# Weight sums in small pieces between products, a reordered start, and a conversion whose last step is put off

## The chip, the cores and the metric

The kernel runs on one core of one Trainium2 chip. Times are device microseconds (us) of one execution. A profile is one execution, taken by the hardware profiler. Engine names in it: PE is TensorE (matrix products), PEld its weight loads, DVE is VectorE, ACT is ScalarE, POOL is GpSimd, SP issues DMAs. `L406` is a line of the kernel of that run, so the same operation has another line number in another kernel; each part below gives the names.

A ratio is the mean time of one kernel's fast runs over that of the other's fast runs of the same rounds on the same chip. It is not quite the ratio of the medians that stand beside it.

## The reference, cut to what matters

```python
# attention: batch 8, heads 8, sequence 576, head size 64; no softmax
scores = q @ k.T / 8 ; ret = scores * decay(h) ** (i - j) for j <= i ; o = ret @ v
# bridge: x is (4608, 512)
# feed-forward with three first weights and a maximum
h   = max(x @ w1, x @ w2, x @ w3)        # 512 -> 768
out = h @ w_out                          # 768 -> 512
```

The weights arrive as 64-bit floats and have to be converted on the chip; all arithmetic is fp32.

## The kernel before

Attention runs in 36 chunks of 128 rows, each with steps transposes, scores (products s and kv) and values (products o). The feed-forward runs in 9 tiles of 512 tokens. Tile 0 uses plain products ("up", "down") while the weights are still being converted. Tiles 1 to 8 use a Strassen-like scheme of seven products per "unit" (a pair of weight blocks, 9 units in a tile) and of seven products for the last matrix (dx, dy, dz). That scheme needs sums of weight blocks (T), of the last weight (To), and of hidden blocks (H).

A unit, cut. Note that product 3 adds into the PSUM tile `x` that the sum after product 5 reads:

```python
product(5, x, False)
nc.vector.tensor_tensor(c22, x[:], p7[:], op=ALU.add)     # L434: VectorE must read x ...
yield
product(4, z, False)
...
product(3, x, False)                                      # ... before this may start
```

The conversion of one piece of a weight, cut:

```python
nc.vector.tensor_scalar(out=expo, in0=high, scalar1=0x7FF00000, op0=bitwise_and)   # mask
nc.scalar.activation(mant, low, Identity, ...)
nc.scalar.activation(expo, expo, Relu, ...)
nc.vector.tensor_scalar(out=frac, in0=high, scalar1=0xFFFFF, op0=bitwise_and)      # mask
nc.scalar.activation(expo, expo, Relu, ...)
nc.vector.scalar_tensor_tensor(out=mant, in0=frac, ..., in1=mant)
nc.vector.scalar_tensor_tensor(out=expo, in0=high, ..., in1=expo)                  # "finish"
nc.gpsimd.tensor_tensor(w, mant, expo, op=mult)                                    # the weight
```

The sums of the last weight and of the hidden blocks stood in one run at the end of a unit:

```python
nc.vector.tensor_tensor(t1, b12, b11, op=subtract)        # 128x768 each
nc.vector.tensor_tensor(t2, b22, t1, op=subtract)
nc.gpsimd.tensor_tensor(b12, b22, b12, op=subtract)
nc.gpsimd.tensor_tensor(t4, b21, t2, op=subtract)
```

## Time and profile before

| | before |
|---|---|
| median of 3 runs | 856.88 us (856.82 to 857.43) |
| TensorE busy | 97% |
| first up product starts | 31.54 us |
| first down product starts | 108.96 us |
| first product of tile 1 | 139.00 us |
| last product ends | 851.86 us |

The table is a set of milestones on TensorE. Because TensorE is nearly always busy, a change shows as the distance between two milestones growing or shrinking. The first up products, from TensorE's timeline (start, duration, operation, count, idle time before and what ended it):

```profile
31.54 7.13 PE L461 MATMUL up<-xT,w 128*128 128x512 f32 x16 [0.43 <-DVE xT L218]
```

Two groups of the conversion are needed later. The view is the groups of instructions by line; columns are count, then busy us and mean ns of one, then idle time before:

```profile
L273 DVE TENSOR_SCALAR frac<-bits 128x512 int32<-128x512 int32 x24 | 25.7, 1071 | 0.0
...
L268 DVE TENSOR_SCALAR expo<-bits 128x512 int32<-128x512 int32 x24 | 13.3, 556 | 0.0
```

The two masks do the same work, and yet one takes twice the time of the other. In the old order GpSimd's product of the piece before is running when frac comes.

### The profile page before, as it was taken

Reading aid. Unit: us, or ns where it says so; the run is one execution under the profiler, and the core shown is the slowest. Engines: PE = TensorE matmul, PEld = TensorE weight load, DVE = VectorE, ACT = ScalarE, POOL = GpSimd, SP = SyncE. Lnnn points to the kernel's source line nnn. Section 1 sums busy time; section 2 is a strip of 40 time slices with the busy share of each in tenths; the row PEclk is TensorE's granted clock in tenths of the full one; section 3 lists DMA queues with packets and bytes.
Section 4 is the critical chain, followed back from the end, with each engine's and each line's share of the span. In section 5 each row is a group of like instructions: output and inputs, shape, how many; then the busy total and the mean of one; then the engine's idle time right before and its main releaser. Section 6 shows DMA issues by size and latency. Waiting matters only on the chain.

```text
span 855.4 us, 12581 instructions
## 1 busy us (share of the span) xinstructions
PE 831.4 (97%) x4608; PEld 669.8 (78%) x4608; DVE 448.2 (52%) x803; ACT 172.8 (20%) x391; POOL 189.4 (22%) x178
## 2 busy tenths in 40 slices
PE   7999989799999999999999999999999999999998
PEld 5645546678888888888888888888888888888887
DVE  4899945745445544555454535554355535543341
ACT  2555631111011111111111111111111111111211
POOL 3534423423302211111211121112021201201000
PEclk9999999989999999999999999999999999999999
DMA  9655531333023322334133323332333223301001
GB/s 245 171 151 160 182 65 51 55 55 75 17 59 74 59 54 54 55 58 83 49 57 54 64 67 55 56 55 68 66 56 54 49 61 69 58 13 38 1 1 49
DMA packets 232509, 59.06 MB, mean 69 GB/s; under 512 B 213504, under 2 KB 230912, under 8 KB 232448
## 3 DMA queue, kind: packets, MB, share of 16 engines
q1 hardware_dynamic: 232016, 57.74, 30.2%
q8 instruction: 36, 0.59, 0.3%
q10 hardware_dynamic: 432, 0.53, 0.2%
q14 instruction: 25, 0.20, 0.1%
HBM read 48.76 MB, written 9.44 MB: 68 GB/s over the span
## 4 chain that ended last, share of the span: by engine, by line
PE 79%; DVE 8%; SPq 5%; ACT 4%; issue 3%; DMA 1%; POOL 0%; DVEq 0%
PE x L406 26%; PE z L406 12%; PE dx L342 9%; PE y L406 6%; PE dz L342 5%; PE s L181 4%; SPq L141 4%; PE o L211 4%; PE o L216 3%; PE kv L192 3%; PE dy L342 2%; PE down L452 2%; ACT expo L271 2%; ACT expo L275 1%; DVE expo L279 1%
## 5 line engine op out<-in xcount | busy, mean ns | idle before, releaser
L406 PE MATMUL x<-S,T 128*128 128x256 f32 x576 | 147.9, 379 | 0.0
L406 PEld LDWEIGHTS x<-S,T 128*128 128x128 f32 x576 | 109.1, 190 | 15.4 <-ACT u L411 0.3
L151 POOL TENSOR_TENSOR vd<-vraw,gk 128x512 f32<-128x512 f32 x36 | 38.6, 1072 | 350.9 <-DMA vraw<-in_v_dram 315.7
L406 PE MATMUL x<-S,w 128*128 128x256 f32 x288 | 76.2, 387 | 8.6 <-DVE h L434 8.5
L434 DVE TENSOR_TENSOR tmp<-x,p 128x256 f32<-128x256 f32 x48 | 20.4, 425 | 104.8 <-PE x L406 104.8
L406 PE MATMUL x<-xT,w 128*128 128x256 f32 x288 | 74.9, 382 | 0.0
L406 PE MATMUL z<-xT,T 128*128 128x256 f32 x288 | 74.0, 379 | 0.0
L406 PE MATMUL y<-xT,w 128*128 128x256 f32 x288 | 73.9, 379 | 0.0
L406 PE MATMUL z<-S,w 128*128 128x256 f32 x288 | 73.9, 379 | 0.0
L411 ACT COPY p<-x 128x256 f32<-128x256 f32 x72 | 26.8, 372 | 223.1 <-PE x L406 217.9
L184 DVE TENSOR_TENSOR st<-s,causal 128x512 f32<-128x512 f32 x72 | 46.3, 685 | 44.1 <-PE s L181 44.1
L406 PEld LDWEIGHTS x<-S,w 128*128 128x128 f32 x288 | 49.9, 191 | 24.0 <-DVE h L434 11.1
L461 PE MATMUL up<-xT,w 128*128 128x512 f32 x144 | 63.5, 594 | 0.4 <-DVE xT L218 0.4
L218 DVE TENSOR_TENSOR xT<-o,gq 128x512 f32<-128x512 f32 x36 | 24.8, 689 | 70.1 <-PE o L216 64.2
L406 PEld LDWEIGHTS y<-xT,w 128*128 128x128 f32 x288 | 54.7, 190 | 7.4
L406 PEld LDWEIGHTS z<-S,w 128*128 128x128 f32 x288 | 54.7, 190 | 7.5
L406 PEld LDWEIGHTS z<-xT,T 128*128 128x128 f32 x288 | 53.9, 189 | 8.4 <-ACT p L411 0.3
L406 PEld LDWEIGHTS x<-xT,w 128*128 128x128 f32 x288 | 51.6, 191 | 6.6 <-issue 0.8
L324 POOL TENSOR_TENSOR H<-h 128x256 f32<-128x256 f32 x24 | 22.7, 947 | 150.3 <-DVE h L446 150.3
L461 PEld LDWEIGHTS up<-xT,w 128*128 128x128 f32 x144 | 26.7, 190 | 30.9 <-issue 29.9
L181 PEld LDWEIGHTS s<-qT,kT 64*128 64x128 f32 x576 | 37.2, 198 | 13.9 <-issue 11.4
L424 DVE TENSOR_TENSOR tmp<-y,p 128x256 f32<-128x256 f32 x48 | 20.4, 425 | 51.7 <-PE y L406 51.7
(91 smaller groups left out, 1229.6 us busy)
## 6 DMA issues: line engine op xcount, KB each, us to landing
bits<-in_moe_w_dram SPq DMA_DIRECT2D x18, 512.0 KB, 3.7
out_dram<-osb SPq DMA_DIRECT2D x36, 256.0 KB, 2.1
kraw<-in_k_dram SPq DMA_DIRECT2D x32, 256.0 KB, 3.1
vraw<-in_v_dram SPq DMA_DIRECT2D x32, 256.0 KB, 3.5
qraw<-in_q_dram SPq DMA_DIRECT2D x448, 16.0 KB, 1.8
kxraw<-in_k_dram SPq DMA_DIRECT2D x448, 16.0 KB, 1.8
bits<-in_moe_w_out_dram SPq DMA_DIRECT2D x6, 512.0 KB, 3.5
qraw<-in_q_dram SPq DMA_DIRECT2D x7, 256.0 KB, 4.6
```

Source lines behind the costliest of these rows:

```text
L141: nc.sync.dma_start(t[32 * a:32 * a + 32, :, blk, :], src[b, a // 2::2, pos:pos + 32, 32 * (a % 2):32 * (a % 2) + 32].rearrange("p j i -> ...
L151: nc.gpsimd.tensor_tensor(t[:], raws.pop(("v", g))[:], gk[:].unsqueeze(2).to_broadcast([C, H, D]), op=ALU.mult)
L181: nc.tensor.matmul(s[j][:, p, :], lhsT=kT[r, p, :], rhs=qT[r, p, :], start=True, stop=True)
L184: nc.vector.tensor_tensor(st[:, j], s[j][:], masks[start_of(g)][:].unsqueeze(1).to_broadcast([C, NP, C]), op=ALU.mult)
L192: nc.tensor.matmul(kv[:, p, :], lhsT=pair(kr, p)[r:], rhs=pair(vds[g], p)[r:], start=True, stop=True)
L211: nc.tensor.matmul(o[D * j:D * (j + 1), p, :], lhsT=vr[:, 2 * p + j, :], rhs=st[:, j, p, :], start=(p == 0), stop=(old == 0 and p == NP - ...
L216: nc.tensor.matmul(o[:, p, :old], lhsT=sd[:, p, :], rhs=qT[:, p, :old], start=False, stop=(p == NP - 1), skip_group_check=True)
L218: nc.vector.tensor_tensor(xT[t][:, :, i * C:(i + 1) * C], o[:], gq[:], op=ALU.mult)
L342: nc.tensor.matmul(out[:, m, :], lhsT=hS[n](fp)[:, m * P:(m + 1) * P], rhs=late["T"][n][:, fp, :], start=first and m == 0 and fp == 0, sto ...
L406: nc.tensor.matmul(out[:], lhsT=w[:, d * P:(d + 1) * P], rhs=xS[t][n][:, d, :], start=first and d == 0, stop=d == 1, skip_group_check=True)
L411: nc.scalar.copy(c[:], src[:])
L461: nc.tensor.matmul(ps[:], lhsT=w_sb[i, fb][:, dc * P:(dc + 1) * P], rhs=xT[t][:, dc, :], start=(dc == 0), stop=(dc == NDC - 1))
```

## The change

Its intent: no long run of sums in front of an eviction that TensorE waits for; a warm TensorE clock and earlier q, k, v at the start; and masks of the conversion that do not stand beside GpSimd's product.

```diff
+    late, chores = {}, deque()
+    def chore(n=1):
+        for _ in range(min(n, len(chores))): chores.popleft()()
 ... sums_of_outs: three thirds of 128x256, each a VectorE chore and a GpSimd chore
 ... sums_of_hidden: three chores; chore() after products 1, 6 and 5 of a unit
 def product(n, out, first):                      # dx, dy, dz
-    for m in range(NM):
-        for fp in range(NF // 2):
+    for fp in range(NF // 2):
+        for m in range(NM):
 ... conversion, now one generator over all pieces: in its third step
+            if last:
+                (finish of the piece before; its product on GpSimd; load_weights(1))
-                    convert(5 if n < 4 else 4)
+                    convert(7 if i == 0 else 4)
 ... start
+    warm(9)                                      # identity products; warm(5) follows transposes(0)
     load(0); load(1)
+    (gs and gq are loaded here, from another queue)
     load(2)
-    load_weights(1)
     load(3)
-    load_weights(2)
+    load_weights(2); load(4); load_weights(2)
 ...
     scores(2)
-    load(4); values(2); convert(2); scores(3); decay_values(4); convert(2); values(3); convert(4)
+    scores(3); convert(2); values(2); convert(3); decay_values(4); values(3); convert(3)
```

(Before, convert(4) stood after scores(1) as well.) ScalarE also takes over four kT copies from VectorE, the weight loads get four buffers in place of three, and raw q three in place of four.

## The prediction

> **What bounds the kernel now.** I read the page first (busy shares, the 40 slices), then the table of waits of TensorE, then TensorE's timeline, then VectorE's and GpSimd's timelines at each place where TensorE stood still.
>
> ```profile
> PE 831.4 (97%) x4608; PEld 669.8 (78%) x4608; DVE 448.2 (52%) x803; ACT 172.8 (20%) x391; POOL 189.4 (22%) x178
> ...
> PE   7999989799999999999999999999999999999998
> ...
> PEclk9999999989999999999999999999999999999999
> ```
>
> TensorE is the bound nearly everywhere, so the change can only win where TensorE has a hole or runs slowly. The waits name the holes:
>
> ```profile
> PE x L406 <- DVE h L434: 8.5, 6, 6.8
> PE kt L168 <- DMA kraw<-in_k_dram: 5.0, 2, 4.1
> PE down L452 <- POOL w_out L285: 3.0, 2, 1.9
> PE dx L342 <- DVE h L446: 2.0, 8, 0.3
> ```
>
> They cost more than they say, because products after a hole run at half speed. From TensorE's timeline (start, duration):
>
> ```profile
> 164.85 1.03 PE L406 MATMUL z<-xT,T 128*128 128x256 f32 x4
> 172.67 2.08 PE L406 MATMUL x<-S,w 128*128 128x256 f32 x4 [6.80 <-DVE h L434]
> 174.68 2.08 PE L181 MATMUL s<-qT,kT 64*128 64x128 f32 x16
> 176.69 2.07 PE L192 MATMUL kv<-vd,kraw 128*128 128x128 f32 x8
> 178.55 1.07 PE L406 MATMUL x<-xT,w 128*128 128x256 f32 x4
> ```
>
> Four products start every 0.86 us elsewhere, 16 score products take 1.1, 8 kv products 1.0. From 164.85 to 178.55 that would be 0.86 + 0.95 + 1.1 + 1.0 = 3.9 us; it took 13.7. **Hole A costs 9.8 us.** It is in the second token tile, before unit 3. VectorE there:
>
> ```profile
> 162.28 0.94 DVE L297 TENSOR_TENSOR T<-w,w 128x256 f32<-128x256 f32 x1
> 163.25 0.84 DVE L298 TENSOR_TENSOR T<-w,T 128x256 f32<-128x256 f32 x1
> 164.01 1.48 DVE L312 TENSOR_TENSOR To<-w_out 128x768 f32<-128x768 f32 x1
> 165.52 1.36 DVE L313 TENSOR_TENSOR To<-w_out,To 128x768 f32<-128x768 f32 x1
> 166.81 2.02 DVE L322 TENSOR_TENSOR H<-h 128x256 f32<-128x256 f32 x1
> 168.86 1.90 DVE L323 TENSOR_TENSOR H<-H,h 128x256 f32<-128x256 f32 x1
> 170.69 0.70 DVE L162 STREAM_TRANSPOSE kT<-kxraw 128x512 f32<-128x512 f32 x1
> ```
>
> The last seventh-product reuses the PSUM tile that L434 must read first, and L434 stands in line behind all these sums.
>
> Hole B: the last products of the first tile wait for converted last weights. TensorE from 108.96 to 121.43 is 12.5 us; it holds 12 down products of 512 columns (0.43 each, 5.2), 1.1 and 1.0: 7.3. **Hole B costs 5.2 us.** Holes C: eight times dx waits for h (0.25 shown, 0.41 by start-to-start against the neighbours), 3.3 us; five further waits for L434 after hole A (0.25 to 0.65 by starts), 2.5 us. The start: the first large product begins at 31.54, while the attention work before it (four chunks of s 1.1, kv 1.1, o 1.0, three of state 1.1, ten groups of transposes 0.44: 20.5 us warm) began at 4.11 and could have ended about 7 us sooner. All else is back-to-back products.
>
> **What the Trainium skill says.** "SBUF — State Buffer", Who interferes with whom: VectorE and GpSimd share a port pair; a two-port-mode VectorE operation, or one with two SBUF inputs, blocks against a GpSimd operation that reads SBUF, and whoever issues first keeps it. The trace agrees: a mask alone takes 0.42 us, and under a GpSimd product (91.96 to 93.35)
>
> ```profile
> 91.80 0.42 DVE L268 TENSOR_SCALAR expo<-bits 128x512 int32<-128x512 int32 x1
> 92.13 1.50 DVE L273 TENSOR_SCALAR frac<-bits 128x512 int32<-128x512 int32 x1
> ```
>
> "TensorE: Matmul & The Clock Gate", What's actually happening: an idle window of about 3.4 us drops the clock to half. The trace agrees: 6.80 us idle, then 2.08 for 1.03. The same page, Architectural detail: VectorE's queue is strictly first in, first out; that is hole A. "DMA: Bandwidth & Descriptors", Issuing engines are not separate DMA queues: transfers interleave whichever engine issued them; so gq and gs, on ScalarE's queue, delay the first q and k. The trace shows the DMA share at 0.90 in the first 10 us, and no more than that.
>
> **The change part by part.**
> 1. *Last-weight sums and unit sums as chores.* The work stays; the order against the evictions changes. At hole A, VectorE's line from its copy of unit 2 (164.01, end of the T pair) to L434 becomes: transposes 1.24, one third of the last-weight sums (two of 128x256 at about 0.43, and up to 0.9 of GpSimd's weight sums in the way), y eviction 0.3 to 0.4, L434 0.4: done at about 167.0 to 167.9. TensorE needs it at 165.7. I leave a loss of 1.8, and 0.4 for a possible clock dip: saved 9.8 - 2.2 = 7.6 us. The rest of the last-weight sums falls in units 3 and 4, each behind an eviction that has 2 to 4 products' time before the next. In the other tiles the two hidden sums still stand before the critical L434 (the chore slots are after products 1 and 6), but GpSimd's two now come after it: 0.55 + 0.88 (their means) becomes about 0.42 x 2, 0.6 us less, which covers waits of 0.25 to 0.65: saved 2.3 of 2.5.
> 2. *dx with the hidden pair as the outer loop.* The last h is needed after 8 matmul records instead of 4: 4 x 0.216 = 0.86 later, more than 0.41. Saved 3.3 us. This is the surest part.
> 3. *Conversion with the finish put behind the next piece's masks.* Before, 80 steps run between products, and one whole piece and more is left at 108.9; after, 98 of 100 steps are issued by then, and only two STT finishes and one mant lie behind the last product. But VectorE has to do it: 23 pieces between about 29 and 112. Per piece before, from 31.4 to 115.3, 83.9 us less 7.3 (12 maxima) less 7.3 (attention) over 22 pieces: 3.15, with 0.3 of it idle for ScalarE. After, the idle goes; but mant, with two SBUF inputs, now starts beside GpSimd's product, and the mask behind it waits for that product. I estimate 0.69 + 0.69 + 1.3 + 0.4 = 3.08. The last w_out is then ready at about 29 + 1.3 + 22 x 3.08 + 14.6 + 1.3 = 114.0; TensorE asks at 108.96 + 10 x 0.43 = 113.3. A short wait without a clock dip: saved 4.2 of 5.2.
> 4. *The start.* Nine identity products (18 records at the cold 0.27 us) warm the clock from about 1.6 to 6; the transposes then take 0.44 instead of 1.09, and s starts at about 9.1 instead of 10.12, kv at 10.2 instead of 11.8. Without gq, gs and the first weight in front, k, q, v of chunks 0 to 3 come earlier, so attention for chunk 3 and the transposes of chunk 4 end at about 28, not 31. But the first weight is then loaded after chunk 3 and converted only behind scores of chunk 3: after xT of chunk 3 (27.9) still frac 0.33, STT 0.61, and GpSimd's product, which mant holds up, 1.8: 30.8. TensorE then idles nearly 3 us where it was busy. Saved: 31.5 - 30.8 = 0.7 us.
> 5. *kT copies to ScalarE, buffers 4 to 3 for q, WAHEAD 4*: nothing by themselves. The tail (last copy, last store) is unchanged.
>
> Sum: 7.6 + 2.3 + 3.3 + 4.2 + 0.7 = 18.1 us; 856.9 - 18.1 = 838.8, said as 838.5.
>
> **Rivals.**
> - *The conversion becomes the bound in the first tile.* VectorE was busy 71.6 of 77.4 us there. If GpSimd's products block more than I think (3.3 per piece), the last weights come 5 us late with a clock dip, hole B stays, and the time is about 843. Against it: frac's mean before, 1.07 us where 0.42 is the mask alone, says that most products blocked a mask already.
> - *The start gains all of it.* If the first weight lands and converts sooner, up to 2.5 us more: 836. Against it: VectorE's new order puts STT of the first piece behind xT of chunk 3.
> - *Hole A only shrinks and still drops the clock.* A hole of 2 to 3 us with GpSimd's sums behind it costs up to 4: 841. For it: the two holes of 1.14 and 1.90 in hole B were enough to lower the clock to 0.93.
> - *Chores make new holes.* A chore behind product 5's eviction delays z's by up to 0.9 us; z's buffer is not needed for a whole unit. I give it little: +1.
> - *Everything goes right*: 21 us of holes and 2 at the start: 834.
>
> **Range and chances.** The holes sum to 20.8 us outside the start, so under 832 is nearly excluded, and nothing that I see makes it slower. Within 2% ends at 839.7, a saving of 17.1, only 1 us from my sum; the errors of parts 1, 3 and 4 are about 1, 1.7 and 1.2 us, together some 2.5 to 3. So 832.5 to 844.5 for 8 in 10; faster by over 2% 0.62, within 2% 0.37, slower 0.01.
>
> **What would show it.** Part 2: no wait of dx for L446 at all. Part 1: in the second tile one wait of x for L434's successor of 1 to 2.5 us where 6.8 stood, and no half-speed products. Part 3: down's wait for w_out under 1.5 us in all. Part 4: kv of chunk 0 at about 10.2; the first up product at 30 to 32, waiting for GpSimd's w. The mean of the expo mask over 1 us and of frac near 0.4 would show the lock moved from one mask to the other, not gone. I am wrong if TensorE waits for w inside the first tile's up products, or if its clock falls below 0.9 after 20 us.

## The result, and the profile after

The changed kernel took 847.25 us (median of 4 runs, 846.79 to 847.83) beside 857.15 for the kernel before: ratio 0.9882, 95% interval 0.9865 to 0.9899. It is faster by 1.2%, where 2.1% was predicted, and lies outside the predicted range; "within 2%" had been given a chance of 0.37.

| milestone on TensorE, us | before | after | stretch before | stretch after |
|---|---|---|---|---|
| first up starts | 31.54 | 33.40 | 31.54 | 33.40 |
| first down starts | 108.96 | 114.33 | 77.42 | 80.93 |
| thirteenth down record starts (hole B lies in here) | 121.43 | 127.19 | 12.47 | 12.87 |
| last product ends | 851.86 | 841.57 | 730.4 | 714.4 |

So the first tile lost 5.8 us, and everything behind it gained 16.0. TensorE's waits of the changed kernel (who waited for whom: us in total, times, longest):

```profile
PE up L483 <- POOL w L385: 4.7, 1, 4.7
PE down L474 <- POOL w_out L385: 3.4, 2, 2.6
...
PE x L425 <- DVE h L455: 1.4, 2, 0.7
```

The waits of dx for h are gone, the 6.8 us wait of x has become two of 0.7, and a new one of 4.7 us leads the list. At hole A, TensorE's timeline after (L425 is the line of the unit products):

```profile
170.61 1.03 PE L425 MATMUL z<-xT,T 128*128 128x256 f32 x4
172.31 1.13 PE L425 MATMUL x<-S,w 128*128 128x256 f32 x4 [0.67 <-DVE h L455]
173.37 1.16 PE L183 MATMUL s<-qT,kT 64*128 64x128 f32 x16
174.47 1.16 PE L194 MATMUL kv<-vd,kraw 128*128 128x128 f32 x8
175.46 1.03 PE L425 MATMUL x<-xT,w 128*128 128x256 f32 x4
```

The same stretch that took 13.70 us takes 4.85, and nothing in it runs at half speed. The new hole before the first up:

```profile
28.15 0.60 PE L173 MATMUL qt<-ident,qraw 128*128 128x128 f32 x4
33.40 8.83 PE L483 MATMUL up<-xT,w 128*128 128x512 f32 x16 [4.66 <-POOL w L385]
```

Sixteen up records took 7.13 us before; 8.83 here means that the first of them ran at half speed after the hole (the granted clock was 0.81 from 33.4 to 42.2 us). The chain that ended last, followed back, names what stood in front of that product (start, length, what):

```profile
24.67 1.10 PE o L218 x8
...
25.87 0.69 DVE state L199
...
26.89 1.41 DVE frac L375
...
31.03 0.61 DVE expo L379
...
31.70 1.65 POOL w L385
...
33.40 5.41 PE up L483 x8
...
38.84 0.02 ACT h L486
...
39.32 0.77 ACT mant L370
...
40.11 0.04 DVE mant L391
```

Three things are to be seen. VectorE's state update at 25.87 comes after products of values(2) (o L218). The frac mask takes 1.41 us in the chain, beside a GpSimd product. And after the up product, the conversion of the next pieces goes on only when ScalarE has copied that product: the copy stands ahead of `mant` in ScalarE's line. VectorE's own waits:

```profile
DVE expo L369 <- POOL w L385: 16.2, 15, 1.2
...
DVE mant L391 <- ACT mant L370: 5.4, 1, 5.4
DVE expo L369 <- POOL w_out L385: 4.6, 4, 1.2
DVE state L199 <- PE o L218: 2.0, 1, 2.0
```

VectorE waits 20.8 us in all (16.2 + 4.6) for GpSimd's product before the first mask of a piece. No such line exists in the profile before. The groups that answer to those of before:

```profile
L369 DVE TENSOR_SCALAR expo<-bits 128x512 int32<-128x512 int32 x24 | 12.8, 534 | 20.8 <-POOL w L385 16.2 <-POOL w_out L385 4.6
...
L375 DVE TENSOR_SCALAR frac<-bits 128x512 int32<-128x512 int32 x24 | 11.2, 466 | 0.0
```

The frac mask fell from 1071 to 466 ns, so the masks are indeed away from GpSimd's product: because VectorE now stands still until it is done. The 14.5 us that frac gave back came back as 20.8 us of waiting.

### The profile page after: what moved, and what is told of

Read it like the earlier page. It is cut to its first block, busy times and chain, and to the rows that moved or that the text cites. A ratio compares the mean times of both kernels' runs of the same rounds, so it can differ in the third digit from the quotient of the medians.

```text
span 845.1 us, 12652 instructions
## 1 busy us (share of the span) xinstructions
PE 830.1 (98%) x4636; PEld 672.6 (80%) x4636; DVE 414.4 (49%) x803; ACT 175.0 (21%) x395; POOL 189.8 (22%) x182
## 4 chain that ended last, share of the span: by engine, by line
PE 86%; DVE 6%; POOL 4%; issue 1%; SPq 1%; DMA 0%; ACT 0%; DVEq 0%; POOLq 0%
PE x L425 28%; PE z L425 14%; PE dx L312 10%; PE y L425 7%; PE dz L312 5%; PE s L183 4%; PE o L213 4%; PE kv L194 4%; PE o L218 4%; POOL w L385 3%; PE dy L312 2%; PE down L474 2%; DVE expo L379 2%; DVE expo L369 1%; SPq L146 1%
## 5 line engine op out<-in xcount | busy, mean ns | idle before, releaser
L425 PE MATMUL x<-S,T 128*128 128x256 f32 x576 | 147.8, 379 | 0.0
L425 PEld LDWEIGHTS x<-S,T 128*128 128x128 f32 x576 | 109.2, 190 | 15.2
L425 PE MATMUL x<-S,w 128*128 128x256 f32 x288 | 74.6, 381 | 1.4 <-DVE h L455 1.4
L425 PE MATMUL x<-xT,w 128*128 128x256 f32 x288 | 74.8, 382 | 0.0
L425 PE MATMUL z<-S,w 128*128 128x256 f32 x288 | 73.9, 379 | 0.0
L425 PE MATMUL z<-xT,T 128*128 128x256 f32 x288 | 73.9, 379 | 0.0
L425 PE MATMUL y<-xT,w 128*128 128x256 f32 x288 | 73.9, 379 | 0.0
L483 PE MATMUL up<-xT,w 128*128 128x512 f32 x144 | 65.8, 609 | 4.8 <-POOL w L385 4.7
L425 PEld LDWEIGHTS x<-S,w 128*128 128x128 f32 x288 | 49.3, 189 | 15.2 <-DVE h L455 2.4
L425 PEld LDWEIGHTS z<-S,w 128*128 128x128 f32 x288 | 54.7, 190 | 7.4
L425 PEld LDWEIGHTS y<-xT,w 128*128 128x128 f32 x288 | 54.7, 190 | 7.4
L425 PEld LDWEIGHTS z<-xT,T 128*128 128x128 f32 x288 | 54.0, 189 | 8.2
L425 PEld LDWEIGHTS x<-xT,w 128*128 128x128 f32 x288 | 51.5, 190 | 6.6 <-issue 0.8
L295 POOL TENSOR_TENSOR H<-h 128x256 f32<-128x256 f32 x24 | 18.6, 774 | 150.4 <-DVE h L468 150.4
L430 ACT COPY u<-x 128x256 f32<-128x256 f32 x72 | 26.8, 372 | 99.9 <-PE x L425 99.9
```

The source lines that it names most:

```text
L425: nc.tensor.matmul(out[:], lhsT=w[:, d * P:(d + 1) * P], rhs=xS[t][n][:, d, :], start=first and d == 0, stop=d == 1, skip_group_check=True)
L430: nc.scalar.copy(c[:], src[:])
L483: nc.tensor.matmul(ps[:], lhsT=w_sb[i, fb][:, dc * P:(dc + 1) * P], rhs=xT[t][:, dc, :], start=(dc == 0), stop=(dc == NDC - 1))
```

## The experiments

My theory after the result: the sums and the dx order bring some 16 us; the new start and the conversion with the postponed finish give about 6 of it back, through three rings and lines. First, two state tiles: scores(3) now stands before values(2), so the state for chunk 4 has to wait until TensorE has read state 2. Second, two `expo` tiles: the mask of piece n+1 overwrites the tile that GpSimd's product of piece n-1, only just issued, still reads. Third, ScalarE's strict order at the first up. Rivals: the parts need each other, so they cannot be summed; the port shared by VectorE and GpSimd stands behind the tile and would cost the same; the loads set the start.

The control of each ratio is the kernel before, on the same chip. Medians of the kernel before were 857.2 to 859.0 us, so ratios are compared, not medians. The 95% interval of a ratio reaches 0.0013 to 0.0025 to either side; that is 1 to 2 us.

| run | median us | ratio to before | first up | up stretch | hole B stretch |
|---|---|---|---|---|---|
| after | 847.25 | 0.9882 | 33.40 | 80.93 | 12.87 |
| after_again | 848.46 | 0.9888 | 35.04 | 82.20 | 13.33 |
| a_dx | 854.81 | 0.9955 | 31.34 | 77.42 | 12.46 |
| a_sums | 843.05 | 0.9811 | 31.83 | 77.42 | 12.42 |
| b_head_conv | 862.15 | 1.0033 | 33.44 | 81.67 | 12.82 |
| c_state3 | 844.76 | 0.9838 | 31.05 | 80.98 | 13.29 |
| d_expo3 | 846.47 | 0.9847 | 33.70 | 79.10 | 10.06 |
| f_oldconv | 845.11 | 0.9846 | 31.54 | 86.01 | 9.08 |
| h_dveprod | 840.78 | 0.9791 | 33.91 | 79.12 | 7.33 |
| q_oldconv_dve | 849.12 | 0.9888 | 32.08 | 89.82 | 7.33 |
| p_sums_dve | 854.29 | 0.9946 | 37.05 | 82.08 | 15.57 |
| j_early_dve | 837.50 | 0.9755 | 32.47 | 77.42 | 7.33 |
| j_again | 837.43 | 0.9745 | 31.17 | 79.12 | 7.33 |
| k_j_nowarm | 837.28 | 0.9752 | 33.00 | 77.42 | 7.34 |
| m_late_vd | 837.44 | 0.9747 | 31.02 | 79.12 | 7.33 |

("Up stretch" is from the first up to the first down, "hole B stretch" from the first down to the thirteenth down record, both from the profile. 7.33 us of the latter is what it takes without a hole. Every experiment gave correct results.)

### a_sums and b_head_conv: the change in two halves

a_sums is the kernel before with the chores and the dx order alone; b_head_conv is the changed kernel with the old sums and the old dx order.

```diff
 # a_sums, on the kernel before
+ chores, chore() after products 1, 6, 5; dx with fp outside m
 # b_head_conv, on the changed kernel
- chores; dx with fp outside m
+ sums_of_outs, sums_of_hidden in one run, dx with m outside fp
```

> The kernel before with only the two parts that the trace says worked: sums as chores, and dx with the hidden pair outside. Theory (the gain is all in these two, and the new start and conversion give 5 to 6 us of it back): hole A saves 8.9 us, the later tiles 7.2, together 16: about 841 us, faster than the changed kernel. Rival (the parts need each other: without the new conversion the chores collide as the old sums did): about 847 or more.

> The changed kernel with the old sums and the old dx order: new start and new conversion alone. Theory: they cost 5 to 6 us, so about 863 us, slower than before. Rival (they are neutral or gain): 857 or less.

a_sums: 0.9811 (0.9796 to 0.9826), 843.05 us. It needs neither the new start nor the new conversion and beats the changed kernel; the rival falls. Its first tile is that of the kernel before, milestone by milestone. b_head_conv: 1.0033 (1.0016 to 1.0049), 862.15 us: slower, as the theory had it, but by 2.8 us and not by 5 to 6. The two ratios give 1 - 0.0189 + 0.0033 = 0.9844 together, against 0.9882 measured for the whole; the halves ran on one chip and the whole on others. With the sums and the dx order in place, the new start and conversion cost 0.9882 - 0.9811, about 6 us. Between 2.8 and 6 the size of the loss stays open; that it is a loss does not.

### a_dx: the dx order alone

```diff
-            for m in range(NM):
-                for fp in range(NF // 2):
+            for fp in range(NF // 2):
+                for m in range(NM):
```

> The kernel before with the hidden pair as dx's outer loop and nothing else. Theory: the eight waits of dx for h go, 8 x 0.41 = 3.3 us, ratio about 0.996. Rival (the copies that then start later hold up the next product): the waits go and others come, ratio 1.000.

0.9955 (0.9942 to 0.9968), that is 3.9 us of 859, with 3.3 inside the interval. Its profile has no wait of dx for h. The chores are then worth about 16.2 - 3.9 = 12 us.

### c_state3: a third state tile

```diff
-    stp = ... tile_pool(name="stp", bufs=2)
+    stp = ... tile_pool(name="stp", bufs=3)      # qT 2 buffers in place of 3, to make room
```

> The changed kernel with three state buffers (qT two instead of three to make room). Theory: VectorE's 1.99 us wait for the products that still read state 2 goes, the first up starts at about 31.5 instead of 33.4, and the time falls by 2 to 4 us, to about 844. Rival (the first weight's own chain or its load sets the start): the wait goes, the first up stays within 0.5 us of 33.4, the time stays at 847.

The first up:

```profile
31.05 8.83 PE L483 MATMUL up<-xT,w 128*128 128x512 f32 x16 [2.58 <-POOL w L385]
```

VectorE's wait for state is gone, and the first up starts 2.35 us sooner. The start varies from run to run, so the hole in front of it says more: 4.66 us in after, after_again and d_expo3, and 2.58 here, which is the wait of 2.0 us and hardly more. (d_expo3 has the same cut of qT, so that cut is not the reason.) The ratio fell from 0.9882 to 0.9838, about 3.8 us by the median of before; that is within what was expected, but in the two profiles the thirteenth down starts only 1.87 us sooner (125.32 for 127.19), so some 2 us of the 3.8 are not traced and lie within the intervals. The ring of state tiles was on the path. The up stretch (80.98) and hole B (13.29) are unchanged, so this ring explains the start alone.

### d_expo3: a third expo tile

```diff
-            expo = wtmp.tile([P, DM], I32, tag="expo", name="expo")
+            expo = wtmp.tile([P, DM], I32, tag="expo", name="expo", bufs=3)   # qT 2 buffers
```

> The changed kernel with three expo buffers (qT two). VectorE now waits 20.8 us in all for GpSimd's product to free the expo tile. Theory 1 (the ring of two tiles sets the 3.13 us per piece): the wait goes, the piece falls to about 2.6 us, hole B shrinks by 2 us or more, about 843 us. Theory 2 (behind the tile stands the shared port, as the prediction had it): the wait goes but the expo mask grows from 0.53 to about 1.4 us in the mean, the piece stays at 3.1 us, the time stays within 1 us of 847.

The wait for GpSimd is gone, and the mask has grown:

```profile
L369 DVE TENSOR_SCALAR expo<-bits 128x512 int32<-128x512 int32 x24 | 29.1, 1210 | 0.0
...
L375 DVE TENSOR_SCALAR frac<-bits 128x512 int32<-128x512 int32 x24 | 12.7, 531 | 0.0
```

534 ns became 1210: 16.3 us of the 20.8 us of waiting turned into 16.3 us of a blocked mask. The mask is held up beside GpSimd's product all the same. That is theory 2; that it is the shared port, and nothing else of the two engines, is read from the prediction's citation and not shown apart. One piece took 3.03 us (the finish at 41.62 to the next at 44.65) in place of 3.13. Theory 1 has one point left: the small gain per piece adds up, and hole B's stretch fell from 12.87 to 10.06. The ratio, 0.9847 (0.9828 to 0.9866), overlaps that of the changed kernel at the edge; some 3 us may be read from it, with little certainty, and the profile is of its fastest run (843.67 us; the others took 846.45 to 847.07). The wait had nearly the same price per piece as the block, so the change could win little by trading one for the other.

### after_again, f_oldconv, h_dveprod, j_early_dve: which order, which engine

after_again is the changed kernel itself on the chip of these three.

> The changed kernel itself, as the control for the three beside it: runs on different chips differed by up to 2 us. Both theories: 1.0 to 1.3% below the kernel before.

0.9888. Its profile shows a first up at 35.04 instead of 33.40; there TensorE also waited 1.5 us for a load of q that it did not wait for in the first profile. It is the profile of the slowest of the four runs (850.61 us; the others took 847.66 to 848.96). The start thus varies by more than a microsecond from run to run.

```diff
 # f_oldconv, on the changed kernel: finish each piece before the next
-            if last: (finish and product of the piece before)
+            (finish and product of this piece, in its fourth step)
```

> The changed kernel with the old conversion, a piece finished before the next is begun, on the new schedule of steps. Theory (the postponed finish loses at the start, because eight steps finish one piece and not two, and gains nothing later, because it only trades a blocked mask for a wait): the first up starts 1.5 to 2 us sooner, at about 31.6, the frac mask is back at about 1.07 us, and the time falls by about 2 us against the control. Rival (the postponed finish is worth its 0.3 us per piece): the last weights come later, hole B grows by 3 us or more, and the time rises.

0.9846, 3.6 us below its control, with the first up at 31.54 and frac at 1338 ns. The time fell as the theory had it. But hole B did not stay either: it shrank to 9.08, while the up stretch grew by 5 us, with attention products waiting for VectorE (4.4 us in all). Undoing the order removed a part of the loss, at the start, and moved another part from hole B into the up stretch.

```diff
 # h_dveprod, on the changed kernel
-                nc.gpsimd.tensor_tensor(w, m[:], e[:].bitcast(FP32), op=ALU.mult)
+                nc.vector.tensor_tensor(w, m[:], e[:].bitcast(FP32), op=ALU.mult)
```

> The changed kernel with the conversion's last product on VectorE in place of GpSimd. Theory (the port that VectorE and GpSimd share costs more than the work GpSimd takes over): no wait for GpSimd and no blocked mask, a piece takes about 2.5 us of VectorE in place of 3.1, hole B goes, first up about 1 us sooner: 840 us, 6 us below the control. Rival (VectorE has no time for 24 more products of 0.69 us, 16.6 us in all): hole B grows, 850.

0.9791, 840.78 us: 8.3 us below the control by the ratios, 7.7 by the medians. VectorE's timeline in the first tile:

```profile
88.58 0.69 DVE L379 SCALAR_TENSOR_TENSOR expo<-bits,expo 128x512 int32<-128x512 int32 x1
89.31 0.69 DVE L385 TENSOR_TENSOR w<-mant,expo 128x512 f32<-128x512 f32 x1
89.92 0.69 DVE L391 SCALAR_TENSOR_TENSOR mant<-frac,mant 128x512 f32<-128x512 int32 x1
90.53 0.42 DVE L369 TENSOR_SCALAR expo<-bits 128x512 int32<-128x512 int32 x1
90.86 0.42 DVE L375 TENSOR_SCALAR frac<-bits 128x512 int32<-128x512 int32 x1
91.20 0.69 DVE L379 SCALAR_TENSOR_TENSOR expo<-bits,expo 128x512 int32<-128x512 int32 x1
```

From finish to finish 2.62 us, with one more operation in it than before and nothing waiting. Giving the busier engine more work made the piece shorter, because that work costs VectorE 0.6 us and the help of GpSimd had cost it 1.1. Hole B is gone: 7.33. The first up did not move sooner here (33.91, with a wait for a load of q in front), but the hole before it shrank from 4.66 to 3.66 us, the one microsecond that was expected.

```diff
 # j_early_dve: h_dveprod with three state tiles (qT two), and
-    scores(3); convert(2); values(2); convert(3); decay_values(4); values(3); convert(3)
+    convert(2); scores(3); convert(2); values(2); convert(3); decay_values(4); values(3); convert(1)
```

> The same product on VectorE, with three state buffers (qT two) and the first two conversion steps before the scores of chunk 3, two more before the values of chunk 2. Theory: the first up follows the transposes without a hole, at about 28.6, at full clock; with hole B gone too: 831 to 835 us, faster than both kernels. Rival (the start is bound by loads of weights, not by order): first up at 31 or later with a wait for a weight's load, 837 or more.

0.9755, 837.50 us, and again 0.9745 as j_again: faster than both kernels by a clear margin, though not 831 to 835. These are the rival's numbers, but not for its reason: no weight's load is waited for. In this profile the up stretch is back at the 77.42 of the kernel before (in j_again it is 79.12, with the first up products partly at half speed again), hole B is closed, but a hole of 2.27 us stays before the first up, now with VectorE's xT as the last thing waited for. In VectorE's line there, a mask still takes 1.50 us at 24.00, beside GpSimd's product for the state.

### k_j_nowarm: without the identity products

```diff
-    warm(9)
-    warm(5)
```

> The fastest so far, repeated as the control for the two beside it: ratio about 0.9755, some 837 us.

> The same without the 14 identity products. Theory (they bring the attention forward, but VectorE's conversion of the first weight, not TensorE, decides when the first up begins): transposes and scores of chunk 0 run at half speed again, the first up starts within 1 us of the control's, the time is within 1 us of it. Rival (the clock is what the start needs): 1.5 to 3 us slower.

0.9752 (0.9739 to 0.9765) beside 0.9745 (0.9730 to 0.9760) for j_again: no difference. The reason expected does not hold, though: the first up starts at 33.00, 1.83 us later than in j_again, and the hole before it is 2.27 us in both, so VectorE's line to the first weight moved along with the attention. The times agree because the sixteen up records took 7.13 us here and 8.83 in j_again; start and duration add up to 40.13 and 40.00 (39.60 in j_early_dve and 39.85 in m_late_vd). So in these four profiles an earlier first up was about paid back in half-speed products. Why is not shown.

### p_sums_dve and q_oldconv_dve: the product on VectorE with the old order

p_sums_dve is a_sums with the product on VectorE: old start, old conversion order, old schedule.

> The kernel before with the sums as chores, the dx order and the conversion's product on VectorE: old start, old conversion order, old schedule of steps. Theory (the new start and the postponed finish are worth nothing once the port is out of the way): hole B falls from 5.2 to under 2.5 us, first up at about 31, 838 to 840 us. Rival (the new schedule, 98 of 100 steps before the downs, is what closes hole B): hole B stays near 5, 842 us.

0.9946, 854.29 us: neither theory. Its first up starts at 37.05, and three waits for the last weights, 5.2 us in all, stand in its downs. A further run was to say whether the old start or the old order did this. q_oldconv_dve is h_dveprod with the old order of conversion, and differs from it in that alone.

> The changed kernel with the product on VectorE and each piece finished before the next; against h_dveprod (0.9791) only the order differs. Theory (without GpSimd the postponed finish is worth VectorE's wait for ScalarE, 0.4 us and more per piece): VectorE waits about 9 us in all for ScalarE's expo, hole B is back with 3 us or more, ratio 0.985 or above. Rival (the slow run was slow by its old start): ratio 0.979 as with the postponed finish.

0.9888 (0.9873 to 0.9903) against 0.9791 of h_dveprod: the order alone is worth 8.3 us once the product is on VectorE. Its waits (the first is TensorE's, the second VectorE's):

```profile
PE o L213 <- DVE st L186: 6.3, 5, 3.1
```

```profile
DVE expo L376 <- ACT expo L372: 7.5, 14, 1.7
```

VectorE's finish waits for ScalarE's part of the same piece, 7.5 us in all. With the old order the finish, the product and the next masks all stand behind that wait. The cost is not where I expected it: hole B is closed (7.33), but the up stretch is 89.82, 10.7 us longer than in h_dveprod, because VectorE falls behind and attention products wait for it. So the postponed finish is a gain without GpSimd's product, and costs 3.6 us with it. The runs that differ from the changed kernel in these two things alone, as ratios:

| | finish postponed | piece finished first |
|---|---|---|
| product on GpSimd | 0.9882, 0.9888 | 0.9846 |
| product on VectorE | 0.9791 | 0.9888 |

The two edits need each other: in the old order, moving the product to VectorE costs 3.6 us. In the kernel with the old start it cost more (p_sums_dve 0.9946 beside a_sums 0.9811, 11.6 us), so of p_sums_dve's loss the old start and its schedule of steps have a part too, 0.9946 - 0.9888 or 5 us; which of the two was not tested.

### m_late_vd: a miss

```diff
-    decay_values(4); values(3); convert(1)
+    values(3); convert(1); decay_values(4)
```

> The fastest so far with GpSimd's vd of chunk 4 issued after the first weight's product. Theory (the masks of the second piece lose 1.3 us under vd): these two masks take 0.42 each, the first up starts about 1.3 us sooner against the transposes' end, ratio about 0.973. Rival (the transposes' copies or the loads follow close behind): first up unchanged, ratio 0.975.

0.9747, no change, and the two masks take 0.89 and 1.26 us as before. The edit does nothing: each engine runs its own line, and GpSimd's line has nothing else in that place, so vd starts when its data are there, wherever it stands in the program. The experiment does not tell the theories apart.

## Why the prediction was wrong

What held, by its own steps:

- Part 1, hole A: 7.6 us predicted, 13.70 - 4.85 = 8.85 measured. Two terms were too cautious: the first third of the last-weight sums took 0.42 and 0.43 us with no GpSimd sum in its way, and the clock did not dip.
- Part 2, dx, and the later tiles together: 5.6 predicted; from the end of hole A to the last product the kernel before took 673.3 us and the changed one 666.1, so 7.2. dx alone measured 3.9 for 3.3.

- Of the signs: dx no longer waits for h, hole A keeps one wait of 0.67 us and no half-speed product, and kv of chunk 0 starts at 10.03 for 10.2. The others failed: down waits 3.4 us for w_out in place of under 1.5, the first up comes after 32, and the means of the masks are 0.53 and 0.47 us, so the lock did not move from one mask to the other; it became a wait. The clock did fall below 0.9 after 20 us (0.81 behind the hole before the first up).

These two were predicted as 13.2 and gave 16.0. The failure lies in the two other parts, predicted to gain 4.9 us and in fact a loss of 5.8. The sum would have missed by 10.7 us, had the first two not given 2.8 more than predicted.

**Part 4, "xT of chunk 3 (27.9) still frac 0.33, STT 0.61, and GpSimd's product, which mant holds up, 1.8: 30.8".** The finish of the first piece started at 30.95 and the first up at 33.40. The last terms were right (they add up to 30.64, not 30.8): from frac at 30.61 to the end of GpSimd's product at 33.34 it took 2.73 us, and predicted were 2.74. It was xT of chunk 3 that came 2.7 us late, because of what stood before it. I had counted VectorE's instructions in their new order and their port, and not asked which tile each of them writes. With scores(3) ahead of values(2), the state for chunk 4 takes the place of state 2, which TensorE reads until 25.8: 1.99 us of waiting in front of the first mask. c_state3 shows it: with a third tile the wait goes, and the hole before the first up falls from 4.66 to 2.58 us. The rest of the difference is the frac mask, which met GpSimd's state product (1.50 us; I had 0.42). The hole of 4.66 us then brought a cost that had no term in the sum: half-speed products, 8.83 - 7.13 = 1.7 us.

**Part 3, "After, the idle goes".** It did not go: VectorE waits 20.8 us for GpSimd through the two expo tiles. The size per piece was nearly right, 3.13 for 3.08, but not for the reason given, and d_expo3 shows why the figures agree: without the ring the port takes 16.3 of these us. What made the last weight late was what came before and between. My sum, with what was measured in it: 114.0 for the last weight, + 2.0 (the finish at 30.95 and not at about 28.9), + 5.4 (ScalarE's copy of the late first up ahead of mant, no term in my sum), + 22 x 0.05 = 122.5; measured 121.12 + 1.26 = 122.4. Since the down products came later too, at 114.33, hole B kept its size and no more: 12.87 for 12.47. My rival "the conversion becomes the bound in the first tile" named this place; its reason, 3.3 us per piece, did not occur.

I had given "the start gains all of it" and "it gains 0.7" as the choices; that the start could lose was in no line. It is shown that the state ring cost about 2 us of the start and that the product on GpSimd cost the conversion its time. Argued from the chain of waits, and not isolated by a run, is the 5.4 us behind ScalarE's copy; the other profiles bear it out, since this wait follows the first up records: 5.4 us where these took 8.83 (after, c_state3), 6.1 where they took 9.52 (b_head_conv), 6.7 where they took 10.12 (after_again). Open is how the loss of the first tile (5.8 us between two profiles, 2.8 us by b_head_conv, 6 us by a_sums) splits to the last microsecond, since the start itself varies by more than one.

## What to carry to other kernels

When work is reordered, write down for every moved instruction which buffer it overwrites and who still reads it; a mask moved away from a busy port into a ring of two tiles waits about as long. Before giving work to a second engine, ask what it costs the first in blocked time: here 0.6 us of VectorE's own work was cheaper than 1.1 us of being blocked or waiting, and only then did putting the finish off pay. The answer holds for one order of work alone: with each piece finished first, the same move of the product cost time. And test the parts of a change one by one: here two parts had all of the gain, and the rest, which cost time as it stood, turned into a gain of some 5 us with further edits (j_early_dve 0.9755 beside a_sums 0.9811; h_dveprod's 0.9791 is not clear of the latter).

## What the Trainium skill lacked or had wrong

- "TensorE: Matmul & The Clock Gate", What's actually happening, has the clock drop after an idle window of about 3.4 us and says that the window runs freely; under HAM oscillation the page makes of it the rule to have no idle gap above about 3.4 us. As a safe length that is too long here: a hole of 2.27 us was enough in one profile and not in another of the same kernel, for sixteen up records took 8.83 us after it in j_again and 7.13 in j_early_dve. That it differs from run to run fits a window that runs freely; that it happens at all does not fit a wholly idle window of 3.4 us, which has no room in such a hole. No run here shows what the length is.
- "SBUF — State Buffer", Who interferes with whom, has VectorE and GpSimd hold each other up, and the masks agree (0.42 us alone, 1.50 beside GpSimd's product); but it does not say who comes next when three operations queue for the port. In d_expo3 mant ran, then GpSimd's product, then the mask: VectorE's next operation did not overtake the waiting product, and took 1.50 us for 0.42, while GpSimd's product was recorded as 1.65 for 1.27.
